# Full-height projections, a split-off negation and a re-ordered plan in a linear-attention kernel with two matrix layers

## The chip, the cores and the metric

The kernel runs on one core of a Trainium2 chip. A core has five engines with a queue of instructions each: TensorE (PE in the profile; its weight loads are PEld) multiplies matrices out of the on-chip memory SBUF into the eight banks of the accumulator memory PSUM; VectorE (DVE) and ScalarE (ACT) do the elementwise work; GpSimd (POOL) here reduces over partitions; SyncE (SP) issues transfers. Engines wait for one another through semaphores. The metric is device time in microseconds.

## The reference

Four batches of eight heads with 576 tokens of 64 numbers pass through an attention with exponential features, then through two dense layers without a bias:

```python
def phi(x):
    proj = np.einsum('bhsd,df->bhsf', x, w_phi)              # 64 -> 128 features
    proj = proj - np.max(np.abs(proj), axis=-1, keepdims=True)
    return np.concatenate([np.exp(proj), np.exp(-proj)], axis=-1)
q_p, k_p = (phi(q), phi(k))
kv = np.einsum('bhsf,bhsd->bhfd', k_p, v)
z = np.sum(k_p, axis=2)
num = np.einsum('bhsf,bhfd->bhsd', q_p, kv)
den = np.einsum('bhsf,bhf->bhs', q_p, z)[..., None] + 1e-06
x = num / den                                                # (2304 tokens, 512)
h = x @ w_in;  x = np.maximum(0.01 * h, h) @ w_out           # layer 1, 512 -> 2048 -> 512
h = x @ w_in2; r = np.maximum(h, 0.0); out = (r * r) @ w_out2
```

The weights of both layers come as 64-bit floats.

## The kernel before

Heads go in pairs: 16 pairs (batch b, pair p), for each of which `k_pair` makes the sums over the keys and `q_pair`, twice, the outputs of half of the tokens (288). Layer 1 (`moe`) goes over five blocks of up to 512 tokens, and in each over 16 pieces of 128 hidden features; it is the longest stretch of matmuls, and attention of batches 1 to 3 runs between its pieces. Layer 2 (`h_unit`, `y_unit`) multiplies by seven products in place of eight, in sweeps over 768 tokens. Weights are turned from 64-bit floats into two rounded halves on DVE and ACT (`w_float`, `w_split`: the tiles `raw`, `wf`, `arena`, `more`, `room`), and products there take three matmuls (high by high, high by low, low by high); those of batch 0 that are called `plain` take one in full precision, which the profile records as two.

In `k_pair` the keys come as a tile of 640 columns: four tiles of 128 tokens with both heads of the pair in the 128 partitions, and a fifth with the 64 left-over tokens of both heads side by side in columns 512 to 639 of partitions 0 to 63; partitions 64 to 127 are zero there. `proj` multiplies tile and weights (`wst`, or its halves `wbh` and `wbl`); for the fifth tile it takes 64 rows. `center` (DVE, lines 1144 and 1145) takes the largest magnitude of each token out of PSUM and negates it, as one step of the plan; `expo` (ACT, line 1151) makes exp(p - max) and exp(max - p) for each head, the tile `kp`; `kv` adds the products of `kp` and the values `vt`. Groups of such tiles are in `KGROUPS`: five groups a pair in batch 0, three in the others.

In `q_pair` the queries `qt` have the same 64 numbers in both halves of the partitions. In batch 0 `proj` multiplies 64 of the rows with `wst`; later `split_a` rounds the whole tile to `qs` (ACT) and `split_b` (DVE) overwrites partitions 64 to 127 with what the rounding lost. Copies `qps`, a reduction over partitions (POOL), exponentials `qe`, their halves, numerator, denominator and its reciprocal (`qden`) follow, and the quotient is split into `xr`, the input of layer 1.

The order of everything is made before the program is: every step is given to a `Plan` with the engines that can take it, an estimated cost and a position. `Plan.order` plays the plan through: each engine, when free, takes the ready step of the lowest position. A step that two engines can take (`{"ACT": (cost, 0), "DVE": (cost, late)}`) counts for the second as so much later. Where TensorE would be idle in the first 95 planned us, `fill` puts a dummy matmul of zeros. The table `P` holds the positions and some costs. What comes out is a fixed sequence for each engine and for SP's queue.

Of the kernel before, what the change touches and what calls it, by code (L numbers as in the profile page):

```python
# [49 lines left out]
P = dict(  # L50
    ring=6, wf=2, raws=3, k0=-165.76, kz=(-19.68, -14.1, -59.35), kp0=15.85, kp=18.51, ks=2.09, kvd=5.48, kb=0, pk=0, pq=0, pn=1, qk=4.25, qk2=11.43,
    q20=-3.11, qd=(1.81, -37.07, 36.76, 8.18, -8.56, -29.92, 30.17), wlead=24.29, wl0=-21.05, ydelay=16.3, xs=(158.38, 39.23, 44.87), xl=58.09,
    xk=58.54, xk2=-16.08, xst=79.13, xld=28.02, lead=37.21, slead=-20.84, w2lead=1.95, ylead=83.28, evac=-13.25, stage0=-49.27, stage=17.12,
    stage2=-17.13, pl=-2.21, c_alt=3.92, sq_alt=14.19, klead=22.1, qlead=14.62, hi_alt=-1.06, dve_alt=42.44, port=1.25, lat=0.125, self=0.115,
    of_pe=0.2, to_pe=0.46, far=0.28, issue=0.47, dma=2.5, rate=320e3, kvc=0.405, switch=0.096, stick=2.0, fill=95, cold=4.98, coldf=2.2,
)
# [185 lines left out]
def attention_moe_moe(ctx: ExitStack, tc: tile.TileContext, qd, kd, vd, wpd, wd, out):  # L242
# [132 lines left out]
    def dves(n, **k):  # L375
        return {"DVE": (on_dve(n, **k), 0)}
# [148 lines left out]
    def stage_pair(p, pos, side):  # L525
# [21 lines left out]

        gate_late.append(plan.add(dves(QD, ops=4), pos - 0.6, comb, r=[f0, f1], w=[sv]))

# [155 lines left out]
    def x_build(i, pos, direct):  # L705
# [6 lines left out]
        for it in range(2 * T // X):  # L712
# [21 lines left out]
            load(512 * 4 * X, pp - P["xl"], get, w=[rv], after=gate_late + need)  # L734
            plan.add(dves(X, ops=4), pp, comb, r=[rv], w=[tv])
            for z, (m0, v, srcs) in enumerate((
# [59 lines left out]
    def h_unit(n):  # L796
# [73 lines left out]
        for c in range(2):  # L870

            def square(e, c=c):
                v = g_tiles[u % UP][:, c]
                if e == "DVE":
                    nc.vector.scalar_tensor_tensor(out=v, in0=v, scalar=0.0, in1=v, op0=ALU.max, op1=ALU.mult)
                else:
                    nc.scalar.activation(out=v, in_=v, func=ACTF.Relu)
                    nc.scalar.activation(out=v, in_=v, func=ACTF.Square)

            plan.add({"ACT": (on_act(2 * T, ops=2), 0), "DVE": (on_dve(2 * T), P["sq_alt"])}, pp + 1 + 0.1 * c, square, p=[g], after=ends[c])  # L880

    def y_unit(n):
# [40 lines left out]
        ops = readers[u % UP]  # L923
        ops.append(plan.add(dves(T, ops=4), pos, comb, r=[gv], w=[sv]))
        for y in range(2):
# [163 lines left out]
    def k_pair(b, p, tpos):  # L1089
# [32 lines left out]
        for tiles, pos in KGROUPS[b > 0]:  # L1122
            pos = tpos[0] + P["ks"] * pos
            heads = [(tt, h) for tt in reversed(tiles) for h in range(1 if tt == 4 else 2)]
# [3 lines left out]
            def proj(e, tiles=tiles, pr=pr):  # L1128
                for y, tt in enumerate(reversed(tiles)):
                    sl, rows, n = (slice(512, 640), slice(0, 64), 128 if plain else 256) if tt == 4 else (slice(tt * 128, (tt + 1) * 128), slice(0, 128), 256)  # L1130
                    ws = [w[rows, 0:n] for w in (wst[:, 128:384], wbh, wbl)]
                    o = banks[pr.bank][:, 256 * y:256 * y + n]
                    if plain:
                        mm(o, t["k"][rows, sl], ws[0], True, True, skip_group_check=True)
                    else:
                        mm(o, t["kh"][rows, sl], ws[1], True, False, skip_group_check=True)
                        mm(o, t["kl"][rows, sl], ws[1], False, False, skip_group_check=True)
                        mm(o, t["kh"][rows, sl], ws[2], False, True, skip_group_check=True)
# [8 lines left out]
            def expo(e, m=m, pr=pr, u=u):  # L1147
                u["kp"] = new("kp", [128, 2, 4, 128], F32)
                for h in range(m):
                    for s, sg in ((0, 1.0), (1, -1.0)):  # L1150
                        nc.scalar.activation(  # L1151
                            out=u["kp"][:, s, h, :], in_=banks[pr.bank][:, h * 128:(h + 1) * 128], func=ACTF.Exp,
                            scale=sg, bias=u["mx"][:, s, h, :],
                        )

# [12 lines left out]

            cost = sum((0.415 if plain else 0.36) if tt == 4 else 0.536 if plain else 0.36 for tt in tiles)
            plan.add(pe(cost), pos, proj, r=[wsv, kt] if plain else [wcv, *ksrc], w=[pr])  # L1170
            plan.add({"DVE": (m * 128 * 1.04e-3 + 0.25, 0)}, pos + 0.4, center, r=[pr], w=[mx]).shared = False
            plan.add({"ACT": (0.5 * m, 0)}, pos + 0.8, expo, r=[pr, mx], w=[kp])
            plan.add(pe((P["kvc"] + 0.02 * (m > 2)) * m), pos + P["kvd"] + P["ks"] * (len(tiles) - 1), kv, r=[kp, vt], w=[acc])
        pos = tpos[-1] + P["kvd"] + 0.1
        f = Value("kvh" if plain_n else "kvf")
# [31 lines left out]
    def q_pair(i, p, pos):  # L1207
        b, c = divmod(i, 2)
        plain, plain_n = b <= P["pq"], b <= P["pn"]
        D8 = P["qd"]  # L1210
        fvals, ft = kvv[b, p]
# [10 lines left out]
        else:  # L1222
# [11 lines left out]
            plan.add(dves(576), pos - 1.5, split_b, r=[qt], w=[qs])  # L1234
        for h in range(2):
            pr = trans(b, False)

            def proj(e, h=h, pr=pr):
                o = banks[pr.bank][:, 0:HALF]
                if plain:  # L1240
                    mm(o, wst[0:64, 0:128], t["q"][0:64, h, :], True, True)
                else:
                    mm(o, w2h, t["qs"][:, h, :], True, False)
                    mm(o, w2l, t["qs"][:, h, :], False, True)
# [5 lines left out]

            plan.add(pe(0.66 if plain else 0.343), pos + D8[0] * h, proj, r=[wsv if plain else wcv, src], w=[pr])
            plan.add({"ACT": (on_act(HALF, psum=True), 0), "DVE": (on_dve(HALF), P["dve_alt"])}, pos + D8[0] * h + 0.2, cp, r=[pr], p=[ps])

# [106 lines left out]
    for b in range(B):  # L1360
        for p in range(PAIRS):
            if b == 0:
                tp = P["k0"] + P["kp0"] * p
            else:
                tp = at[NCH * (b - 1)] + P["kz"][b - 1] + P["kp"] * p
            todo.append((tp - 12, 0, "k", (b, p, [tp + P["ks"] * o for o in range(5)])))
            for c in range(2):
                qp = tp + P["qk"] + P["qk2"] * c + (P["q20"] * c if b == 0 else 0)
                todo.append((qp - 12, 1, "q", (qp, 2 * b + c, p)))
# [92 lines left out]
```

## Time and profile before

| | us |
|---|---|
| median of three runs | 977.25 (975.85 to 987.81) |
| the profiled execution, its own time | 976.32 |
| its span | 974.6 |
| PE busy | 957.0 |
| PEld busy | 862.9 |
| DVE busy | 775.2 |
| ACT busy | 562.0 |
| POOL busy | 92.6 |

The span runs from the first to the last instruction; the rest of the time lies around it. Busy is the time in which an engine had an instruction in work. Matmuls of PE overlap, so PE counts as busy also where they follow each other with small delays. The granted TensorE clock was 0.999 of full speed. A row "out<-in" names the tile written and those read; "64\*128" is rows by columns of the weights, "128x288" the shape written.

### The profile page before, as it was taken

Reading aid. Unit: us, or ns where it says so; the run is one execution under the profiler, and the core shown is the slowest. Engines: PE = TensorE matmul, PEld = TensorE weight load, DVE = VectorE, ACT = ScalarE, POOL = GpSimd, SP = SyncE. Lnnn points to the kernel's source line nnn. Section 1 sums busy time; section 2 is a strip of 40 time slices with the busy share of each in tenths; the row PEclk is TensorE's granted clock in tenths of the full one; section 3 lists DMA queues with packets and bytes.
Section 4 is the critical chain, followed back from the end, with each engine's and each line's share of the span. In section 5 each row is a group of like instructions: output and inputs, shape, how many; then the busy total and the mean of one; then the engine's idle time right before and its main releaser. Section 6 shows DMA issues by size and latency. Waiting matters only on the chain.

```text
span 974.6 us, 16578 instructions
## 1 busy us (share of the span) xinstructions
PE 957.0 (98%) x5893; PEld 862.9 (89%) x5893; DVE 775.2 (80%) x1628; ACT 562.0 (58%) x1327; POOL 92.6 (9%) x52
## 2 busy tenths in 40 slices
PE   9999999999999999999999999999999999999997
PEld 7788877888888888888888899999999999999997
DVE  6999999999999999995143421779997787878877
ACT  7997878678787879863232332344543434334343
POOL 2331201011212101110000000000000000200201
PEclk9999999999999999999999999999999999999999
DMA  8547978987888578799779399979975294818623
GB/s 273 194 143 269 313 237 293 328 285 273 279 280 303 195 243 281 251 300 365 285 256 335 135 311 336 357 301 286 305 295 210 116 335 171 278 28 305 160 76 66
DMA packets 89010, 244.89 MB, mean 251 GB/s; under 512 B 7776, under 2 KB 32224, under 8 KB 85856
## 3 DMA queue, kind: packets, MB, share of 16 engines
q1 hardware_dynamic: 85616, 239.65, 70.6%
q0 software_dynamic: 3312, 4.20, 2.8%
q8 instruction: 46, 0.75, 0.3%
q14 instruction: 36, 0.29, 0.1%
HBM read 167.00 MB, written 76.81 MB: 250 GB/s over the span
## 4 chain that ended last, share of the span: by engine, by line
PE 56%; DVE 31%; DMA 6%; issue 3%; ACT 3%; SPq 0%; DVEq 0%; ACTq 0%
PE bank L348 56%; DVE qden L1326 3%; DVE s L357 3%; DVE gl L357 2%; DMA raw<-wd 2%; DVE wf L483 2%; DVE room L357 2%; DVE g L991 1%; DVE kmx L1144 1%; DVE raw L478 1%; DVE g L835 1%; DMA wid<-room 1%; DVE qm L357 1%; DMA wsd<-arena 1%; DVE qs L357 1%
## 5 line engine op out<-in xcount | busy, mean ns | idle before, releaser
L348 PE MATMUL bank<-gh,arena 128*128 128x512 f32 (+1 forms) x640 | 200.1, 372 | 0.0
L348 PE MATMUL bank<-xr,arena 128*128 128x512 f32 (+1 forms) x720 | 162.9, 370 | 0.0
L357 DVE TENSOR_TENSOR gl<-g,gh 128x512 fp32r<-128x512 f32 (+2 forms) x176 | 94.2, 539 | 75.0 <-ACT gh L352 74.3
L348 PEld LDWEIGHTS bank<-xr,arena 128*128 128x128 f32 x720 | 124.8, 189 | 21.4
L348 PEld LDWEIGHTS bank<-gh,arena 128*128 128x128 f32 x640 | 117.1, 189 | 19.5
L348 PE MATMUL bank<-gl,arena 128*128 128x512 f32 (+1 forms) x320 | 118.0, 369 | 0.0
L1256 POOL PARTITION_ALL_REDUCE qm<-qps x32 | 75.8, 2369 | 342.2 <-ACT qps L352 231.2
L352 ACT ACTIVATE gh<-g 128x512 fp32r<-128x512 f32 (+2 forms) x157 | 77.5, 501 | 38.6 <-PE bank L348 35.2
L1151 ACT ACTIVATE kp<-bank,kmx 128x128 f32<-128x128 f32 x288 | 79.9, 382 | 16.0 <-DVE kmx L1145 14.2
L348 PE MATMUL bank<-xc,w 128*128 128x384 f32 x504 | 88.7, 334 | 0.0
L646 ACT ACTIVATE g<-bank 128x512 f32<-128x512 f32 (+1 forms) x80 | 44.2, 552 | 76.0 <-PE bank L348 75.7
L348 PEld LDWEIGHTS bank<-xc,w 128*128 128x128 f32 x504 | 87.1, 188 | 0.0
L348 PE MATMUL bank<-arena,sc 128*128 128x256 f32 x648 | 83.3, 282 | 0.2 <-DVE g L839 0.2
L352 ACT ACTIVATE sc<-s 128x256 fp32r<-128x256 f32 (+1 forms) x89 | 45.9, 517 | 62.8 <-DVE s L357 23.7
L348 PEld LDWEIGHTS bank<-arena,sc 128*128 128x128 f32 x648 | 79.8, 188 | 0.6 <-issue 0.3
L348 PEld LDWEIGHTS bank<-vt,kp 128*128 128x128 f32 x576 | 69.7, 191 | 6.2 <-ACT kp L1151 1.7
L348 PE MATMUL bank<-vt,kp 128*128 128x65 f32 (+1 forms) x576 | 70.4, 273 | 1.6 <-ACT qden L1312 1.0
L348 PEld LDWEIGHTS bank<-gl,arena 128*128 128x128 f32 x320 | 60.4, 189 | 8.5
L357 DVE TENSOR_TENSOR sc<-s,sc 128x512 fp32r<-128x512 f32 (+1 forms) x96 | 51.3, 553 | 18.8 <-ACT sc L352 18.8
L835 DVE TENSOR_TENSOR g<-bank,g 128x384 f32<-128x384 f32 x72 | 40.0, 555 | 33.1 <-PE bank L348 27.6
L1326 DVE RECIPROCAL qden<-qden 128x288 f32<-128x288 f32 x32 | 62.3, 1946 | 1.2 <-ACT qden L1312 1.1
L352 ACT ACTIVATE g<-bank 128x384 f32<-128x384 f32 (+2 forms) x60 | 29.0, 483 | 57.6 <-PE bank L348 57.6
(141 smaller groups left out, 1873.7 us busy)
## 6 DMA issues: line engine op xcount, KB each, us to landing
arena<-wsd SPq DMA_DIRECT2D x72, 512.0 KB, 5.0
raw<-wd SPq DMA_DIRECT2D x64, 512.0 KB, 5.3
xc<-xcd SPq DMA_DIRECT2D x28, 768.0 KB, 12.9
arena<-wcd SPq DMA_DIRECT2D x10, 1792.0 KB, 7.4
wsd<-arena SPq DMA_DIRECT2D x28, 512.0 KB, 4.8
wid<-room SPq DMA_DIRECT2D x24, 512.0 KB, 5.1
wcd<-room SPq DMA_DIRECT2D x24, 512.0 KB, 4.7
xcd<-xc SPq DMA_DIRECT2D x14, 768.0 KB, 9.2
```

The costliest lines, as they stand in the source:

```text
L348: nc.tensor.matmul(out=o, lhsT=lhsT, rhs=rhs, start=start, stop=stop, **kw)
L352: nc.scalar.activation(out=out, in_=in_, func=ACTF.Copy)
L357: ENG[e].tensor_tensor(out=out, in0=a, in1=b, op=ALU.subtract)
L478: nc.vector.tensor_scalar(out=low, in0=low, scalar1=29, scalar2=None, op0=ALU.logical_shift_right)
L483: nc.vector.scalar_tensor_tensor(out=t["f"].bitcast(I32), in0=high, scalar=3, in1=low, op0=ALU.logical_shift_left, op1=ALU.bitwise_or)
L646: nc.scalar.activation(out=t["g"], in_=banks[hb.bank][:, 0:N], func=ACTF.Prelu, alpha=0.01)
L835: nc.vector.tensor_tensor(out=t[o], in0=m(z), in1=t["a"], op=ALU.add)
L991: nc.vector.tensor_tensor(out=o, in0=a, in1=b, op=op)
L1144: nc.vector.tensor_reduce(out=mx[1], in_=o, axis=AX.X, op=ALU.max, apply_absolute_value=True)
L1151: nc.scalar.activation(out=u["kp"][:, s, h, :], in_=banks[pr.bank][:, h * 128:(h + 1) * 128], func=ACTF.Exp, scale=sg, bias=u["mx"][:, s, ...
L1256: nc.gpsimd.partition_all_reduce(out_ap=t["m"].rearrange("p h s -> p (h s)"), in_ap=t["ps"].rearrange("p h s -> p (h s)"), channels=128, r ...
L1326: nc.vector.reciprocal(out=t["d"], in_=t["d"])
```

## The change

- The fifth tile of the keys, and the queries of batch 0, are projected with all 128 rows; the weights used have zeros in partitions 64 to 127 where those rows hold something else.
- `split_b` writes the lost parts to partitions 0 to 63 and leaves the rounded numbers in 64 to 127.
- `center` keeps the maximum alone; the negation is a step of its own, `negate`, which ACT or DVE can take, and `expo` is two steps, of which the one with exp(max - p) needs no negation.
- Planned costs of these steps and of the four-part combinations change, and nearly all numbers of `P`, some of them now apart for batch 0. Every order follows from these.

```diff
-    ring=6, wf=2, raws=3, k0=-165.76, kz=(-19.68, -14.1, -59.35), kp0=15.85, kp=18.51, ks=2.09, kvd=5.48, ...
+    ring=6, wf=2, raws=3, k0=-171.94, kz=(-21.52, -26.27, -66.22), kp0=15.74, kp=18.04, ks=2.77, kvd=5.48, ...
...
+    ng_alt=20.3, of_pe=0.2, to_pe=0.46, far=0.28, issue=0.47, dma=2.5, rate=320e3, kvc=0.405, switch=0.096, stick=-15.08, fill=95, cold=4.98,
+    coldf=2.2, qd0=(4.31, -14.43, 40.84, 7.57, 13.97, 1.25, 42.32), ks0=1.47, kvd0=2.9, qk0=4.73,
...
-                    sl, rows, n = (slice(512, 640), slice(0, 64), 128 if plain else 256) if tt == 4 else (slice(tt * 128, (tt + 1) * 128), slice(0, 128), 256)
-                    ws = [w[rows, 0:n] for w in (wst[:, 128:384], wbh, wbl)]
+                    sl, n = slice(tt * 128, (tt + 1) * 128), 128 if plain and tt == 4 else 256
+                    ws = [w[:, 0:n] for w in (wst[:, 128:384], wbh, wbl)]
...
                 nc.vector.tensor_reduce(out=mx[1], in_=o, axis=AX.X, op=ALU.max, apply_absolute_value=True)
-                nc.vector.tensor_scalar(out=mx[0], in0=mx[1], scalar1=-1.0, scalar2=None, op0=ALU.mult)
+
+            def negate(e, m=m, u=u):
+                mx = [u["mx"][:, s, 0:m, :] for s in range(2)]
+                if e == "ACT":
+                    nc.scalar.activation(out=mx[0], in_=mx[1], func=ACTF.Copy, scale=-1.0)
+                else:
+                    nc.vector.tensor_scalar(out=mx[0], in0=mx[1], scalar1=-1.0, scalar2=None, op0=ALU.mult)
...
+            def expo(e, s, m=m, pr=pr, u=u):
+                if "kp" not in u:
+                    u["kp"] = new("kp", [128, 2, 4, 128], F32)
                 for h in range(m):
...
-            plan.add({"ACT": (0.5 * m, 0)}, pos + 0.8, expo, r=[pr, mx], w=[kp])
+            plan.add({"ACT": (0.15, 0), "DVE": (0.075, P["ng_alt"])}, pos + 0.6, negate, r=[mx], w=[mn]).shared = False
+            plan.add({"ACT": (0.25 * m, 0)}, pos + 0.7, lambda e, f=expo: f(e, 1), r=[pr, mx], p=[kp])
+            plan.add({"ACT": (0.25 * m, 0)}, pos + 0.8, lambda e, f=expo: f(e, 0), r=[pr, mx, mn], p=[kp])
...
-                sub(e, r[64:128], t["q"][64:128], r[64:128])
+                sub(e, r[0:64], t["q"][0:64], r[0:64])
...
-                    mm(o, wst[0:64, 0:128], t["q"][0:64, h, :], True, True)
+                    mm(o, wst[:, 128:256], t["q"][:, h, :], True, True)
```

In the printed orders TensorE has 250 dummy matmuls for 209 and otherwise the same matmuls; SP's queue has 471 entries in both, POOL's 55, in the same order. DVE has 1,585 instructions for 1,628: 41 of the 56 negations are ACT's now. Of those 56, 20 belong to batch 0, and 13 of these 20 stay on DVE. ACT has 1,372 instructions for 1,327.

DVE at the end of attention of batch 0, before (`kmx` is the maximum, `qden` the denominator, `xr` the input of layer 1, `kl` the lost part of batch 1's keys):

```order
L1326 RECIPROCAL qden<-qden 128x288
L1144 TENSOR_REDUCE kmx<-bank_76 128x4
L1145 TENSOR_SCALAR kmx<-kmx 128x4
L1329 TENSOR_TENSOR qnum<-qnum,qden 128x288
L483 SCALAR_TENSOR_TENSOR wf<-raw 128x512
L354 CAST xr<-qnum 128x256
L354 CAST xr<-qnum 128x32
```

The same place after the change:

```order
L1336 RECIPROCAL qden<-qden 128x288
L1145 TENSOR_REDUCE kmx<-bank_76 128x4
L1339 TENSOR_TENSOR qnum<-qnum,qden 128x288
L484 SCALAR_TENSOR_TENSOR wf<-raw 128x512
L355 CAST xr<-qnum 128x256
L355 CAST xr<-qnum 128x32
```

The negation between the reduction and the quotient has left DVE's sequence; what follows stands as it stood.

ACT at the first keys of batch 1, before (`kp` the exponentials of the keys, six of them for three heads):

```order
L352 ACTIVATE kvh<-bank_82 128x2x64
L352 ACTIVATE qps<-bank_80 128x288
L352 ACTIVATE kvh<-bank_82 128x2x64
L1151 ACTIVATE kp<-bank_76,kmx 128x128 x6
L474 ACTIVATE raw<-raw 128x512
L1312 ACTIVATE qden<-bank_77 64x288
```

The same keys after the change:

```order
L353 ACTIVATE xr<-qnum 128x224
L1150 ACTIVATE kmx<-kmx 128x3
L1158 ACTIVATE kp<-bank_76,kmx 128x128 x3
L1322 ACTIVATE qden<-bank_75 64x288
L1158 ACTIVATE kp<-bank_76,kmx 128x128 x3
L1322 ACTIVATE qden<-bank_77 64x288
```

The negation stands on ACT right before the exponentials, and these are two runs of three with a denominator of batch 0 between them.

TensorE at the beginning of layer 1, before (`xr,arena` is layer 1, `qs,arena` a query projection of batch 1, `vt,kp` the key sums):

```order
L348 MATMUL bank_75<-vt,kp 128x65 x16
L348 MATMUL bank_76<-qs,arena 128x288 x2
L348 MATMUL bank_77<-xr,arena 128x512 x12
L348 MATMUL bank_75<-qs,arena 128x288 x2
L348 MATMUL bank_78<-xr,arena 128x512 x12
```

And after the change:

```order
L349 MATMUL bank_77<-xr,arena 128x512 x6
L349 MATMUL bank_75<-vt,kp 128x65 x4
L349 MATMUL bank_76<-room,kh 128x256
L349 MATMUL bank_76<-room,kl 128x256
L349 MATMUL bank_76<-room,kh 128x256 x2
L349 MATMUL bank_76<-room,kl 128x256
L349 MATMUL bank_76<-room,kh 128x256
L349 MATMUL bank_77<-xr,arena 128x512 x6
```

Pieces of attention now stand between halves of a piece of layer 1, where before they stood between whole ones.

## Rows read from the trace of the kernel before

**Rows 1.** Stretches: from:to, length, busy us (instructions) by engine, clock, DMA share, GB/s.

```profile
20.00:78.00 58.00, 56.48 (x440) 46.91 (x438) 56.34 (x111) 52.69 (x160) 15.97 (x7) 1.00 0.52 175
78.00:440.00 362.00, 355.59 (x1904) 299.60 (x1903) 350.00 (x661) 285.38 (x723) 55.31 (x23) 1.00 0.82 278
160.00:320.00 160.00, 157.80 (x868) 134.58 (x868) 154.68 (x294) 125.41 (x323) 24.28 (x10) 1.00 0.84 286
440.00:640.00 200.00, 200.00 (x1114) 178.86 (x1113) 81.67 (x172) 67.83 (x125) 0.00 (x0) 1.00 0.82 293
640.00:960.00 320.00, 317.93 (x2265) 315.01 (x2264) 264.46 (x622) 138.85 (x272) 13.60 (x13) 1.00 0.63 215
```

**Rows 2.** Waits, 78 to 440 us: engine, for whom, total us, times, longest.

```profile
PEld bank L348 <- ACT kp L1151: 7.1, 12, 1.4
...
PEld bank L348 <- ACT qps L352: 4.2, 8, 1.7
...
PE bank L348 <- ACT kp L1151: 2.6, 4, 1.0
```

**Rows 3.** Timeline of DVE around a negation: start, us, engine, line, operation.

```profile
108.58 0.41 DVE L1144 TENSOR_REDUCE kmx<-bank 128x2 f32<-128x256 f32 x1
109.03 0.17 DVE L1145 TENSOR_SCALAR kmx<-kmx 128x2 f32<-128x2 f32 x1
109.10 0.45 DVE L1329 TENSOR_TENSOR qnum<-qnum,qden 128x288 f32<-128x288 f32 x1
109.47 0.82 DVE L357 TENSOR_TENSOR kl<-kt,kh 128x640 fp32r<-128x640 f32 x1
```

**Rows 4.** Groups by shape, DVE, 0 to 440 us: busy us, mean ns, idle before.

```profile
L1145 DVE TENSOR_SCALAR kmx<-kmx 128x2 f32<-128x2 f32 x28 | 7.4, 265 | 1.0
L354 DVE CAST gh<-g 128x512 fp32r<-128x512 f32 x13 | 6.6, 506 | 0.8 <-ACT g L646 0.8
L354 DVE CAST arena<-wf 128x512 fp32r<-128x512 f32 x8 | 4.6, 581 | 0.0
...
L1145 DVE TENSOR_SCALAR kmx<-kmx 128x4 f32<-128x4 f32 x12 | 3.6, 301 | 0.4
L354 DVE CAST room<-s 128x512 fp32r<-128x512 f32 x7 | 3.5, 495 | 0.0
L1145 DVE TENSOR_SCALAR kmx<-kmx 128x3 f32<-128x3 f32 x12 | 2.9, 242 | 0.4
```

**Rows 5.** Groups by shape, ACT, 0 to 440 us: its smallest operation.

```profile
L352 ACT ACTIVATE xr<-qnum 128x32 fp32r<-128x32 f32 x3 | 0.7, 234 | 1.2 <-DVE qnum L1329 1.2
```

**Rows 6.** Timeline of PE: projections of 64 rows, and products of 128.

```profile
8.78 0.75 PE L348 MATMUL bank<-qt,wst 64*128 64x288 f32 x2
9.46 0.70 PE L348 MATMUL bank<-wst,kt 128*128 128x256 f32 x2
...
53.52 1.23 PE L348 MATMUL bank<-qt,wst 64*128 64x288 f32 x4
54.68 0.38 PE L348 MATMUL bank<-room,kh 128*128 128x256 f32 x1
...
55.78 2.21 PE L348 MATMUL bank<-qe,kvh 128*128 128x288 f32 x8
57.83 1.90 PE L348 MATMUL bank<-vt,kp 128*128 128x65 f32 x16
```

**Rows 7.** Timeline of PE: a key projection of 128 rows, then dummy matmuls.

```profile
63.74 0.50 PE L348 MATMUL bank<-room,kh 128*128 128x256 f32 x1
64.07 0.28 PE L348 MATMUL bank<-room,kl 128*128 128x256 f32 x1
...
64.65 2.69 PE L348 MATMUL bank<-zeros 128*128 128x128 bf16 x45
67.15 0.51 PE L348 MATMUL bank<-qs,arena 128*128 128x288 f32 x2
```

**Rows 8.** Timeline of PE: the first matmuls of layer 1.

```profile
77.68 2.91 PE L348 MATMUL bank<-xr,arena 128*128 128x512 f32 x12
```

More of the change, by code (lines that the diff above doesn't have):

```diff
@@ L546, in comb @@
                 sub("DVE", q[3], a12, q[1])
-        gate_late.append(plan.add(dves(QD, ops=4), pos - 0.6, comb, r=[f0, f1], w=[sv]))
+        gate_late.append(plan.add({"DVE": (on_dve(QD, ops=4) + 0.118, 0)}, pos - 0.6, comb, r=[f0, f1], w=[sv]))
         def part_of(t, a, m):
@@ L734, in x_build @@
             load(512 * 4 * X, pp - P["xl"], get, w=[rv], after=gate_late + need)
-            plan.add(dves(X, ops=4), pp, comb, r=[rv], w=[tv])
+            plan.add({"DVE": (on_dve(X, ops=4) + 0.118, 0)}, pp, comb, r=[rv], w=[tv])
             for z, (m0, v, srcs) in enumerate((
@@ L878, in square @@
                     nc.scalar.activation(out=v, in_=v, func=ACTF.Square)
-            plan.add({"ACT": (on_act(2 * T, ops=2), 0), "DVE": (on_dve(2 * T), P["sq_alt"])}, pp + 1 + 0.1 * c, square, p=[g], after=ends[c])
+            plan.add({"ACT": (on_act(2 * T, ops=2) + 0.13, 0), "DVE": (on_dve(2 * T) + 0.04, P["sq_alt"])}, pp + 1 + 0.1 * c, square, p=[g], after=ends[c])
     def y_unit(n):
@@ L923, in y_unit @@
         ops = readers[u % UP]
-        ops.append(plan.add(dves(T, ops=4), pos, comb, r=[gv], w=[sv]))
+        ops.append(plan.add({"DVE": (on_dve(T, ops=4) + 0.118, 0)}, pos, comb, r=[gv], w=[sv]))
         for y in range(2):
@@ L1167, in kv @@
                         )
-            cost = sum((0.415 if plain else 0.36) if tt == 4 else 0.536 if plain else 0.36 for tt in tiles)
+            cost = sum((0.26 if plain else 0.36) if tt == 4 else 0.536 if plain else 0.36 for tt in tiles)
             plan.add(pe(cost), pos, proj, r=[wsv, kt] if plain else [wcv, *ksrc], w=[pr])
-            plan.add({"DVE": (m * 128 * 1.04e-3 + 0.25, 0)}, pos + 0.4, center, r=[pr], w=[mx]).shared = False
-            plan.add({"ACT": (0.5 * m, 0)}, pos + 0.8, expo, r=[pr, mx], w=[kp])
-            plan.add(pe((P["kvc"] + 0.02 * (m > 2)) * m), pos + P["kvd"] + P["ks"] * (len(tiles) - 1), kv, r=[kp, vt], w=[acc])
-        pos = tpos[-1] + P["kvd"] + 0.1
+            mn = Value()
+            plan.add({"DVE": (m * 128 * 1.04e-3 + 0.07, 0)}, pos + 0.4, center, r=[pr], w=[mx]).shared = False
+            plan.add({"ACT": (0.15, 0), "DVE": (0.075, P["ng_alt"])}, pos + 0.6, negate, r=[mx], w=[mn]).shared = False
+            plan.add({"ACT": (0.25 * m, 0)}, pos + 0.7, lambda e, f=expo: f(e, 1), r=[pr, mx], p=[kp])
+            plan.add({"ACT": (0.25 * m, 0)}, pos + 0.8, lambda e, f=expo: f(e, 0), r=[pr, mx, mn], p=[kp])
+            plan.add(pe((P["kvc"] + 0.02 * (m > 2)) * m), pos + P["kvd0" if b == 0 else "kvd"] + P["ks"] * (len(tiles) - 1), kv, r=[kp, vt], w=[acc])
+        pos = tpos[-1] + P["kvd0" if b == 0 else "kvd"] + 0.1
         f = Value("kvh" if plain_n else "kvf")
@@ L1209, in q_pair @@
         plain, plain_n = b <= P["pq"], b <= P["pn"]
-        D8 = P["qd"]
+        D8 = P["qd0" if b == 0 else "qd"]
         fvals, ft = kvv[b, p]
@@ L1230, in split_b @@
                 r = t["qs"]
-                sub(e, r[64:128], t["q"][64:128], r[64:128])
+                sub(e, r[0:64], t["q"][0:64], r[0:64])
             plan.add(acts(576), pos - 2, split_a, r=[qt], w=[qs])
-            plan.add(dves(576), pos - 1.5, split_b, r=[qt], w=[qs])
+            plan.add({"DVE": (on_dve(576), 0)}, pos - 1.5, split_b, r=[qt], w=[qs])
         for h in range(2):
```

36 lines of the change are left out of this document (16 added, 20 removed).

## The prediction

> **What bounds the kernel now.** Read the stretches first [rows 1]. In each row the second figure is what TensorE (PE) was busy. From 440 to 640 us PE is busy for 200.00 of 200 us and VectorE (DVE) for 81.67: there TensorE alone sets the pace, and from 640 to 960 us it is busy for 317.93 of 320. Before that it is another kernel. From 78 to 440 us DVE is busy for 350.00 of 362 us and from 20 to 78 us for 56.34 of 58, so 97% in both, while ScalarE (ACT) has 285.38 and 52.69. PE is shown busy there too, but its matmuls are pipelined and overlap in the record; the table of waits says more [rows 2]. In 78 to 440 us the weight loads of PE wait 7.1 us for the exponentials `kp`, and 4.2 us for the query copies `qps`, both made by ACT, and the matmuls wait another 2.6 us for `kp`. So the first 440 us are a pipeline in which DVE has hardly a gap, ACT hands its results over late, and PE waits in small pieces. The rest is bare PE work.
>
> Where does the change act? The printed orders agree from the other end: the last 1,860 matmuls of PE and the last 490 instructions of DVE are the same ones in the same order, and before them, with short pieces exchanged between, stand unbroken blocks of 258 and 672 matmuls that reach back into the later part of layer 1. Nothing that the change does reaches the part after 440 us except by when it begins. So the 535 us from there on are taken over as they are, and everything below is a shift of the point at which TensorE is left to run alone.
>
> **The parts, and what each costs.**
>
> *The negated maximum.* Before, DVE reduces a tile, then negates at once: reduce at 108.58 (0.41 us), negation at 109.03, next operation at 109.10 [rows 3]. Neighbours overlap by 0.08 us (109.10 + 0.45 against 109.47), so without the negation the next would start near 108.91: 0.19 us each. Of the 56 negations 41 go to ACT, which makes 41 x 0.19 = 7.8 us off DVE. By the mean durations of the rows, which hold some that were slowed to over a microsecond, it is 16 x 0.265 + 11 x 0.242 + 11 x 0.301 = 10.2 us for the 38 with two or more heads [rows 4]. Those are the two ends.
>
> *What DVE gets in exchange.* The new order sends more rounding copies to DVE. Counted up to the last split of `xr`, which ends attention: 5 more `room<-s` at 0.495, 4 more `arena<-wf` at 0.581, 4 more `gh<-g` at 0.506 [rows 4]: 2.5 + 2.3 + 2.0 = +6.8 us. The other differences there are one to four instructions each, of both signs, and I cost them at nothing, within 1 us. DVE thus loses between 7.8 - 6.8 = 1.0 us and 10.2 - 6.8 = 3.4 us until attention is done. I take **-2.0**, a little under the middle since the row with the start times is the more direct one. As DVE is 97% busy this counts in full.
>
> *Exponentials.* exp(max - x) needs the maximum alone and no longer waits for the negation, which is 0.19 us earlier for its group. 12 + 4 = 16 waits of PE in 78 to 440 us end on `kp` [rows 2]: at most 16 x 0.19 = 3.0 us, at least nothing, if ACT has other work queued ahead. On ACT itself the nearest small operation is 0.234 us (128x32) [rows 5], so 41 cost it at most 9.6 us. What hides them is ACT's idle time, 362 - 285.38 = 77 us from 78 to 440 us. In the prologue there is little of it (5.3 us of 58), but there 13 of the 20 negations stay on DVE, so ACT gets 7 x 0.234 = 1.6 us. If that cover fails, rival B is what follows.
>
> *Full-height projections.* A lone query projection of 64 rows takes from 8.78 to 9.46, 0.68 us; two in a row take from 53.52 to 54.68, 0.58 each; a product of the same width over 128 rows, eight records for four of them, takes from 55.78 to 57.83, 0.51 each [rows 6]. So 0.07 to 0.17 us for each of 16 query projections and 4 left-over key tiles of batch 0: -1.4 to -3.4. For the 12 left-over tiles of the later batches, six matmuls of which three have 64 rows take from 54.68 to 55.78, 1.10 us [rows 6]; six of 128 rows take from 63.74 to 64.65, 0.91 with a late start, and by the later five of them (64.07 to 64.65) 6 x 0.116 = 0.70 [rows 7]: -0.2 to -0.4 each, -2.3 to -4.8. Together -3.7 to -8.2 us of PE, in the stretch where PE waits for others.
>
> The Trainium skill speaks against this part: TensorEngine Tiling (Array Packing), sections Overview and When to Use Tiling, has contractions of up to 64 run as row tiles, for up to twice the rate. The trace doesn't agree: two 64-row projections in a row were slower than two of 128 rows, 1.16 against 1.02 us. By that rule the 16 projections would cost PE 16 x 0.25 = 4 us instead of gaining, an estimate from half of 0.51, and the sum would be near 978.
>
> *Fillers.* 41 more dummy matmuls stand before the first matmul of layer 1 (250 for 209). 45 of them took from 64.65 to 67.15, 0.056 us each [rows 7]: +2.3 us at most, nothing if they only fill waiting. The first x of layer 1 needs DVE's last split of batch 0 anyway, and in DVE's order less work stands before that one than before, by the negations that left.
>
> *Low half of the queries.* The subtraction keeps its shape, 64 partitions by 576, so its time; nothing, and the products summed are the same in another order.
>
> *The rest of the order* has the same instructions and the same transfers in other places. SP's queue has 471 entries in both, with single loads moved by a few places: nothing, unless a load comes late, which is in rival B's price.
>
> **Sum.** PE's own saving becomes waiting time as long as DVE sets the pace, so DVE's -2.0 is the base. The earlier exponentials, with PE's saving behind them, could add between 0 and 3.0; I take half, -1.5. That makes -3.5 us. The profiled execution took 976.3 us (span 974.6, 1.7 around it), so **972.8 us**; the median of the runs shown is 977.25, 0.9 above that execution. The forecast's own range is 967 to 976.
>
> **Rivals.**
>
> *A. The order closes gaps of its own (faster, about 966).* DVE still idles 1.7 + 12.0 = 13.7 us in 20 to 440 us [rows 1]. If the new order removes the later half of that, and PE's saving and the shorter waits let it, the gain is 3.5 + 7 = 10.5: 966; with all of it 959, which is as far as it goes. For it: PE's, ACT's and DVE's terms all point down, and the waits of [rows 2] are on what gets earlier. Against: DVE at 97% has little left, and a fixed order can't be better than its estimates.
>
> *B. ACT becomes late (slower, about 986).* ACT's order has more work than before in front of the middle units of layer 1: negations, and batch 1's attention taken earlier against its weight work. Priced by durations of the same forms it is 4 us more at the end of attention (36 more instructions, of which 41 negations at most 9.6 us, less the rounding copies that went to DVE), but 10 to 14 us more in front of the activations of 160 to 320 us. ACT's idle time there is 160 - 125.41 = 34.6 us [rows 1]. It decides where that idle time is not where the work lands: then matmuls of layer 1 wait for `gh`, PE loses up to 13, and the forecast's 3.5 come off: +9.5, 986. Against it: 34.6 covers 14. For it: PE's waits already end on ACT, not on DVE. The Trainium skill has a rule on this side too: ScalarE: Activation LUTs, section Rules for kernel authors, puts multiplications on VectorE and not on ScalarE.
>
> *C. Nothing comes through (976).* DVE's saving is eaten by the copies it was given, and the first 78 us, where 13 negations stay where they were, set the start of layer 1.
>
> *D. 64-row tiles were the better ones,* by the rule above: 978.
>
> **Chances.** Forecast 0.55, A 0.17, B 0.17, C 0.09, D 0.02. The range must leave out no more than 2 in 10: it takes the forecast, C and D, most of A (to 963) and most of B (to 983): **963 to 983**. A difference of 2%, which is 19.5 us and about what a measurement of this kernel can tell from no change, would need 957.7 or less, beyond all that A has to give unless PE's saving comes on top: 0.03. Slower by as much, 996.8, would need B's price twice over: 0.04. Within 2%: 0.93.
>
> **What would show it.** In the stretches: 440 to 960 us unchanged in kind, all of the difference earlier. DVE's negations 56 to 15, its busy time to attention's end 1 to 4 us less. Waits of PE for `kp` shorter, none on a 64-row form. B would show as waits of PE for `gh` or `qden` growing between 160 and 320 us. The forecast is wrong if the first matmul of layer 1 starts over 3 us earlier or later than at 77.68 [rows 8], if DVE's idle time before 440 us changes by over 5 us, or if any of the difference arises after it.

## The result, and the profile after

The changed kernel takes 963.97 us (median of four runs, 963.57 to 965.49), against 979.2 us for the kernel before in the same series (median of four, 975.85 to 987.81). The ratio, estimated from the fast runs of both and so not the quotient of these medians, is 0.9854 with an interval of 0.9823 to 0.9885. The profiled execution took 963.57 us (span 961.8) for 976.32 (974.6): 12.8 us less. The forecast was 972.8 in a range of 963 to 983. The direction and the range held, the size did not: it said -3.5 from the profiled execution, and -12.8 came.

The stretches of the kernel after, with the columns of [rows 1]:

```profile
20.00:78.00 58.00, 57.88 (x476) 50.73 (x475) 57.41 (x110) 52.56 (x168) 15.35 (x7) 1.00 0.57 181
78.00:440.00 362.00, 356.81 (x1934) 304.75 (x1933) 348.35 (x648) 290.56 (x755) 54.74 (x23) 1.00 0.86 294
160.00:320.00 160.00, 157.71 (x876) 135.71 (x875) 156.94 (x299) 132.00 (x348) 26.46 (x12) 1.00 0.87 302
440.00:640.00 200.00, 200.00 (x1159) 180.76 (x1158) 78.01 (x158) 68.87 (x131) 0.00 (x0) 1.00 0.78 283
```

The share of DVE is what it was: 57.41 of 58 and 348.35 of 362, for 56.34 and 350.00. A full engine stays full while the work in front of it gets less, so the time is found by matching the same instruction in both traces instead. Starts on TensorE, in us (`xr` matmuls are those of layer 1 that read its input):

| | before | after | shift |
|---|---|---|---|
| first matmul of layer 1 | 77.7 | 72.6 | -5.1 |
| 241st of its `xr` matmuls | 243.3 | 241.0 | -2.3 |
| 481st | 424.6 | 415.2 | -9.5 |
| 529th | 448.0 | 436.9 | -11.1 |
| first of layer 2 | 602.6 | 591.6 | -11.1 |
| last matmul of all | 968.44 | 955.35 | -13.1 |

From the 529th on the shift stays constant to the end of layer 1. Between, it goes up and down because the new order puts attention and layer 1 differently. Layer 2 brings another 2 us.

The waits of the kernel after, 78 to 440 us (engine, for whom, total us, times, longest), first of the weight loads, then of the matmuls:

```profile
PEld bank L349 <- ACT kp L1158: 3.2, 5, 1.6
...
PE bank L349 <- ACT kp L1158: 0.5, 2, 0.3
```

Against [rows 2] the waits for `kp` went from 7.1 + 2.6 to 3.2 + 0.5 us, and those for `qps` from 4.2 to 2.1.

What the negation costs on ACT stands in its timeline (start, us, engine, line, operation):

```profile
105.95 0.19 ACT L1150 ACTIVATE kmx<-kmx 128x3 f32<-128x3 f32 x1
106.04 0.87 ACT L1158 ACTIVATE kp<-bank,kmx 128x128 f32<-128x128 f32 x3
```

It is busy for 0.19 us, but the exponentials start 0.09 us after its own start, since neighbours overlap. The forecast priced it at up to 0.234 from [rows 5].

Full-height projections of queries in the kernel after, alone and two in a row, for those of [rows 6]:

```profile
9.83 0.70 PE L349 MATMUL bank<-qt,wst 128*128 128x288 f32 x2
10.37 1.00 PE L349 MATMUL bank<-vt,kp 128*128 128x65 f32 x8
11.20 0.70 PE L349 MATMUL bank<-qt,wst 128*128 128x288 f32 x2
...
50.58 1.19 PE L349 MATMUL bank<-qt,wst 128*128 128x288 f32 x4
51.61 0.44 PE L349 MATMUL bank<-zeros 128*128 128x128 bf16 x5
```

From start to start one takes 0.54 us (0.68 before) and two take 1.03 (1.16 before). All sixteen together, each to the start of the next other instruction, took 9.81 us before and 8.41 after: -1.4, the low end of the forecast's -1.4 to -3.4 that it gave for queries and plain key tiles together. The matmuls beside a 64-row one take longer too, which neither the forecast nor this sum counts (last section).

### The profile page after: what moved, and what is told of

It is laid out like the page before. It is cut to its first block, busy times and chain, and to the rows that moved or that the text cites. A ratio compares the mean times of both kernels' runs of the same rounds, so it can differ in the third digit from the quotient of the medians.

```text
span 961.8 us, 16628 instructions
## 1 busy us (share of the span) xinstructions
PE 946.5 (98%) x5934; PEld 864.2 (90%) x5934; DVE 762.4 (79%) x1585; ACT 566.7 (59%) x1372; POOL 91.2 (9%) x52
## 4 chain that ended last, share of the span: by engine, by line
PE 59%; DVE 26%; ACT 5%; DMA 5%; issue 3%; SPq 0%; DVEq 0%; ACTq 0%
PE bank L349 59%; DVE qden L1336 3%; DMA raw<-wd 3%; DVE gl L358 2%; DVE wf L484 2%; DVE s L358 2%; DVE room L358 2%; DVE qs L358 1%; DVE g L992 1%; DVE kmx L1145 1%; ACT kp L1158 1%; DVE arena L358 1%; ACT qe L1282 1%; DVE qel L358 1%; DVE raw L479 1%
## 5 line engine op out<-in xcount | busy, mean ns | idle before, releaser
L353 ACT ACTIVATE gh<-g 128x512 fp32r<-128x512 f32 (+2 forms) x152 | 74.5, 498 | 39.0 <-PE bank L349 36.2
L1158 ACT ACTIVATE kp<-bank,kmx 128x128 f32<-128x128 f32 x288 | 84.4, 380 | 2.4 <-issue 1.7
L349 PE MATMUL bank<-arena,gh 128*128 128x256 f32 x324 | 60.8, 283 | 1.3 <-DVE xt L992 1.3
```

Source lines behind the costliest of these rows:

```text
L349: nc.tensor.matmul(out=o, lhsT=lhsT, rhs=rhs, start=start, stop=stop, **kw)
L353: nc.scalar.activation(out=out, in_=in_, func=ACTF.Copy)
L1158: nc.scalar.activation(out=u["kp"][:, s, h, :], in_=banks[pr.bank][:, h * 128:(h + 1) * 128], func=ACTF.Exp, scale=1.0 - 2.0 * s, bias=u[" ...
```

## The experiments

Ratios are to the kernel before, timed in the same series; times are medians. "Shift" is a start in the trace against the kernel after, as in the table. The medians of the kernel before were 977.09 to 979.2 in the five series, so a difference to the kernel after of under 2 us shows little by itself. A shift is that of one execution, which can be the fastest or the slowest of its kernel. Unless one says otherwise, a kernel keeps the order of the kernel it starts from, instruction by instruction.

### Order or operations?

**New operations in the old order.** The kernel before, with full-height projections and the low half, the negation on ACT for batches 1 to 3, and the exponentials exp(max - p) ahead of the others of their group:

```diff
-                nc.vector.tensor_scalar(out=mx[0], in0=mx[1], scalar1=-1.0, scalar2=None, op0=ALU.mult)
+                if b == 0:
+                    nc.vector.tensor_scalar(out=mx[0], in0=mx[1], scalar1=-1.0, scalar2=None, op0=ALU.mult)
...
+                if b > 0:
+                    nc.scalar.activation(out=u["mx"][:, 0, 0:m, :], in_=u["mx"][:, 1, 0:m, :], func=ACTF.Copy, scale=-1.0)
```

> The order of the kernel before, with the operations of the change in it: 128 rows for the left-over keys and batch 0's queries, the low half of the queries, the negation on ACT for batches 1 to 3 (on DVE in batch 0), exp(max - x) ahead of exp(x - max). Theory ORDER (most of the gain comes from the new sequence): 3 us or less are gained, 973 to 977. Rival OPS (the operations themselves bring it): 7 us or more, 969 or less.

969.57 us, ratio 0.9923 (0.9905 to 0.9941), before 977.58: -8.0 without any new order. In its trace the gain grows from 0.7 us at the first matmul of layer 1 to 3.2 at the 241st and 8.2 at the 481st, and stays there; layer 2 takes 0.6 back.

**Old operations in the new order.** The kernel after with the 64-row projections, the high half and the negation in `center` on DVE (`negate` does nothing):

```diff
+                nc.vector.tensor_scalar(out=mx[0], in0=mx[1], scalar1=-1.0, scalar2=None, op0=ALU.mult)
...
-                    mm(o, wst[:, 128:256], t["q"][:, h, :], True, True)
+                    mm(o, wst[0:64, 0:128], t["q"][0:64, h, :], True, True)
...
-                sub(e, r[0:64], t["q"][0:64], r[0:64])
+                sub(e, r[64:128], t["q"][64:128], r[64:128])
```

> The order of the change, with the operations of before in it: 64 rows, the high half, all 56 negations on DVE right behind their maximum. Theory ORDER: 7 us or more of the 12 remain, 969 or less. Rival OPS: it falls back to 973 or more.

975.64 us (median of twelve), 0.9973 (0.9957 to 0.9989): the order alone brings 1.9 us. In the traces, layer 2 from its first to its last matmul takes 365.8 us in the kernel before and 364.1 here, so about 1.7 us of it lie there. Read the other way, the operations are worth 975.64 - 963.97 = 11.7 us in the new order.

**New operations planned with the old table.** The kernel after, planned anew with the numbers of `P` from before (the separate numbers of batch 0 set to the common ones):

```diff
-    ring=6, wf=2, raws=3, k0=-171.94, kz=(-21.52, -26.27, -66.22), ...
+    ring=6, wf=2, raws=3, k0=-165.76, kz=(-19.68, -14.1, -59.35), ...
```

> The change's operations, steps and planned costs with the numbers of the table from before (batch 0's separate numbers set to the common ones, the delay of a negation on DVE as in the change): the order is planned anew from them. Theory TABLE (what the sequence adds to the operations' 8 us, some 5 us, comes from the new numbers): 968 to 971. Rival STEPS (it comes from the negation and the exponentials being steps of their own, and from better costs): 966 or less.

972.51 us, 0.9945 (0.9927 to 0.9963), 8.5 slower than after, and slower also than the new operations in the old order. Its plan has 372 dummy matmuls for 250. The new numbers are worth little with the old operations (1.9) and much with the new ones (8.5): they fit the new operations better. "Order" and "operations" aren't terms that add up.

### Which operation?

**Only the 64-row projections back**, queries and left-over keys, in the kernel after:

```diff
-                        mm(o, t["kh"][:, sl], ws[1], True, False, skip_group_check=True)
+                        mm(o, t["kh"][rows, sl], ws[1], True, False, skip_group_check=True)
...
-                    mm(o, wst[:, 128:256], t["q"][:, h, :], True, True)
+                    mm(o, wst[0:64, 0:128], t["q"][0:64, h, :], True, True)
```

> The change with its 64-row projections put back (16 query projections, 16 left-over key tiles), everything else and the order as in the change. Theory ORDER: TensorE waits in that part anyway, so 0 to +2 us on the change's 964. Rival OPS: +4 us or more, the rows' own 3.7 to 8.2 us in full.

968.86 us, 0.991 (0.989 to 0.9929): +4.9. The first matmul of layer 1 starts at 76.07 for 72.62, +3.5; after that the shift grows only to 4.1. As both traces hold the same matmuls in the same order, the shift can be told apart by where it arises (us, by the start in the kernel after):

| stretch | at 64-row matmuls and their two neighbours | at all others |
|---|---|---|
| 7.4 to 20 | +1.6 | 0.0 |
| 20 to 72.6 | +2.8 | -1.1 |
| 72.6 to 415 | +4.3 | -3.7 |

So the 64 rows cost TensorE 8.7 us. Up to layer 1, 3.3 of 4.4 us stay in the time; after it, beside attention of the later batches, only 0.6 of 4.3, since other matmuls then follow their neighbours sooner.

**Only the left-over key tiles back to 64 rows:**

```diff
-                        mm(o, t["kh"][:, sl], ws[1], True, False, skip_group_check=True)
+                        mm(o, t["kh"][rows, sl], ws[1], True, False, skip_group_check=True)
```

> The change with the left-over key tiles alone put back to 64 rows (16 tiles, 48 matmuls or records of the later batches among them); batch 0's queries keep 128. All rows put back cost 4.9 us, 3.5 of them before layer 1 began. Theory PROLOGUE (TensorE is close to the limit in the first 73 us, and the 16 query projections there carry most): +0.5 to +2 us on 964. Rival COUNT (it goes by the matmuls' own time, of which the 12 later tiles have 2.3 to 4.8 us): +3 us or more.

965.54 us, 0.9877 (0.9861 to 0.9893): +1.6, with the first matmul of layer 1 at 73.37. Of the 3.5 us there, 2.7 are thus the query projections of batch 0. What they are worth at the end isn't settled: by the medians 4.9 - 1.6 = 3.3 us, but the trace of this kernel, the slowest of its five runs, is 3.3 us late at layer 2 where that of all rows is 4.1, which leaves 0.8.

**Only the negation back on DVE**, in `center`:

```diff
+                nc.vector.tensor_scalar(out=mx[0], in0=mx[1], scalar1=-1.0, scalar2=None, op0=ALU.mult)
...
-            def negate(e, m=m, u=u):
+            def negate(e):
+                pass
```

> The change with the negation back on DVE right behind each maximum, everything else and the order as in the change; DVE gets 41 instructions of 0.19 us back, 7.8 us. Theory ORDER: +1 to +4 us on the change's 964, since DVE still has gaps to take them. Rival OPS, by which DVE's work counts in full: +6 us or more.

968.83 us, 0.9912 (0.9894 to 0.993): +4.9. Its shift is +1.1 at the first matmul of layer 1 and grows to +5.4. The two single steps, 4.9 + 4.9 = 9.8, nearly make up the 11.7 of all the operations.

### What does a microsecond cost on each engine?

In the kernel after, work was added whose result nobody uses. **On DVE**, a second negation for each of the 36 groups of batches 1 to 3 (36 x 0.19 = 6.8 us by [rows 3]):

```diff
                 nc.vector.tensor_reduce(out=mx[1], in_=o, axis=AX.X, op=ALU.max, apply_absolute_value=True)
+                if b > 0:
+                    nc.vector.tensor_scalar(out=dead[:, 0:m].rearrange("p (a b) -> p a b", b=1), in0=mx[1], scalar1=-1.0, scalar2=None, op0=ALU.mult)
```

> The change with 36 dead negations on DVE, one behind each maximum of batches 1 to 3, into a tile that nobody reads; ACT's negations stay. 36 x 0.19 = 6.8 us of DVE. Theory TURNS (before 440 us DVE, PE and ACT hold each other up in turn, and work on any of them costs half or more of itself): +3.5 us or more on the change's 964. Rival LATENCY (what putting the negation back cost, 4.9 us, was exponentials that start later): 0 to +1.5 us, as nobody waits for these.

970.51 us, 0.9922 (0.9906 to 0.9938). **On ACT**, 68 negations, two for each group of batches 1 to 3 whose own negation is there (68 x 0.09 = 6 us):

```diff
+                    if b > 0:
+                        for y in range(2):
+                            nc.scalar.activation(out=dead[:, 4 * y:4 * y + m].rearrange("p (a b) -> p a b", b=1), in_=mx[1], func=ACTF.Copy, scale=-1.0)
```

> The change with 68 dead negations on ACT, two behind each of its 34 negations of batches 1 to 3; they take 0.09 us each between their neighbours, 6 us of ACT. Theory TURNS: +3 us or more on 964. Rival ROOM (ACT idles over 70 us from 78 to 440 us and takes such work for nothing): 0 to +1.5 us.

966.89 us, 0.9882 (0.9864 to 0.99). Both hold an error of the edit: the new 32-byte tile `dead` moved other tiles, and layer 1 itself became slower (last section). They were run again, writing into padding that was there already:

```diff
-    dead = const.tile([128, 8], F32, name="dead")
...
-    first.tile([128, EDGE], F32, name="edge")
+    dead = first.tile([128, EDGE], F32, name="edge")
```

> The 36 dead negations on DVE once more (6.8 us of it), now written into a padding tile that was there already, so that nothing moves in SBUF. In the first such run layer 1's matmuls ran 1.8 ns slower each even where neither DVE nor ACT had anything to do with them, about 2 us of its +6.5. Theory TURNS: +3.5 to +5.5 us on the change's 964, and none of it after 430 us. Rival LATENCY: 0 to +1.5 us.

> The 68 dead negations on ACT once more (6 us of it), written into the padding tile. Theory TURNS: +3 us or more on 964. Rival ROOM: 0 to +1.5 us, since about 2 us of the first run's +2.9 arose in the stretch of matmuls alone, from the shift in SBUF.

DVE: 969.54 us, 0.9913 (0.9892 to 0.9934), +5.6 for 6.8 us. ACT: 964.67 us, 0.9869 (0.9852 to 0.9887), +0.7 for 6 us, which can't be told from nothing. Their shifts at layer 2 are +6.6 and 0.0. So ACT has room for such pieces, and DVE hasn't.

**On PE**, each split key projection of batches 1 to 3 repeats its first matmul (60 x 0.12 = 7.2 us by [rows 7]):

```diff
                         mm(o, t["kh"][:, sl], ws[1], True, False, skip_group_check=True)
+                        mm(o, t["kh"][:, sl], ws[1], True, False, skip_group_check=True)
```

> The change with the first matmul of each key projection of batches 1 to 3 made twice (the second overwrites the first): 60 matmuls of 256 columns at 0.12 us, 7.2 us of PE. Theory TURNS: +3.6 us or more on 964. Rival DVE ALONE (the prediction's: PE's work turns into or out of waiting while DVE sets the pace): 0 to +1.5 us.

968.17 us, 0.9897 (0.9879 to 0.9914): +4.2 (shift at layer 2 +5.4, in the slowest of its five runs). TensorE counts too, before 440 us, where DVE is as good as full (348.35 of 362 us in the kernel after). **Dummy matmuls:** of the 250, 106 were left out:

```diff
+        made[0] += 1
+        if made[0] > 38 and made[0] % 2:
+            return
```

> The change with 144 dummy matmuls for 250, every second one after the first 38 left out: 106 x 0.056 = 5.9 us of PE less in the first 73 us. Theory TURNS for the beginning too: layer 1 starts 1 to 4 us earlier, 960 to 963. Rival COVER (they only fill waiting): within 0.5 us of the change's 964.

965.55 us, 0.9873 (0.9853 to 0.9892), +1.6, with intervals of after and this one that overlap. The first matmul of layer 1 comes 0.3 us later, not earlier: the dummies don't hold the start up.

### The rounding copies

The forecast set 6.8 us of copies, which the new order gives to DVE, against the negations that leave it. With the order held fixed, they were given to ACT at the same places: first the `room` copies (14 before 425 us, 6.6 us by their rows), then also those of `arena` (12, 5.4 us), and, apart, the 15 negations still on DVE; last all of it.

```diff
-                copy(e, dst[:, :, 0].bitcast(F32R), src())
+                copy("ACT", dst[:, :, 0].bitcast(F32R), src())
...
-            copy(e, dst()[:, 0].bitcast(F32R), t["f"])
+            copy("ACT", dst()[:, 0].bitcast(F32R), t["f"])
...
-                if e == "ACT":
-                    nc.scalar.activation(out=mx[0], in_=mx[1], func=ACTF.Copy, scale=-1.0)
-                else:
-                    nc.vector.tensor_scalar(out=mx[0], in0=mx[1], scalar1=-1.0, scalar2=None, op0=ALU.mult)
+                nc.scalar.activation(out=mx[0], in_=mx[1], func=ACTF.Copy, scale=-1.0)
```

> The kernel after, in its own order; the rounding copies room<-s and room<-wf that its plan gave to DVE (14 of them before 425 us, 6.6 us by their rows) are emitted for ACT at the same places. Theory (these copies cost what other DVE work costs, 0.8 of their length, and ACT has room at 0.1 to 0.2 of 14 x 0.55): 5.3 - 1.2 = 4.1 us off, about 960. Rival (the planner put them where DVE would have waited anyway, so they cost nothing): 964 to 965. Second rival (ACT is late at those places): over 966.

> As the one with the room copies, and the 12 copies arena<-wf on DVE (5.4 us by their rows) are emitted for ACT as well: 12 us less on DVE, about 14 us more on ACT before 425 us. Theory (0.8 of DVE's work counts, 0.1 to 0.2 of ACT's): 9.6 - 2.1 = 7.5 us off, about 956.5. Rival (the copies sit in gaps of DVE): 964 to 966. Second rival (ACT is late, matmuls of layer 1 wait for arena): 967 to 975.

> The kernel after, in its own order; the 15 negations that its plan left on DVE are emitted for ACT at the same places. DVE gets 15 x 0.19 = 2.9 us less, ACT 15 x 0.09 = 1.4 us more. Theory (DVE's work before 440 us counts at about 0.8, ACT's at 0.1 to 0.2): 2.3 - 0.3 = 2.0 us off the kernel after, about 962. Rival (13 of them lie in the first 78 us, where ACT is as full as DVE and each result is awaited at once): no gain or up to 1.5 us lost, 964 to 965.5.

> Copies and negations of the kernel after all on ACT, at the same places in the order: 15 us less on DVE, 15.5 us more on ACT before 425 us. Theory: the sum of the two, about 954 to 955. Rival (copies in gaps, negations as in the rival there): 964 to 967. Second rival (ACT late): 967 to 977.

`room`: 965.63 us, 0.9883 (0.9867 to 0.9899), +1.7. Both kinds: 968.66 us, 0.991 (0.9895 to 0.9925), +4.7. The 15 negations: 964.67 us, 0.987 (0.9856 to 0.9885), +0.7, no difference that can be told. All: 969.12 us, 0.9917 (0.9902 to 0.9932), +5.2. The shift at the first matmul of layer 2 says the same: +1.0, +4.1, +0.8, +5.5. Nothing is gained by moving 12 us off the fullest engine. The kernel with both kinds of copies on ACT shows why, in the waits of DVE from 20 us to its last split of `xr`, which ends attention:

```profile
DVE room L358 <- ACT room L353: 3.4, 9, 0.6
DVE gh L355 <- ACT g L647: 2.5, 3, 1.7
```

The step that takes the lost part of `room` is on DVE and now waits for the copy from ACT, and other steps of DVE wait for an ACT that is later. In the kernel after, neither wait is over 0.3 us up to there. DVE up to that last split, in all of these traces (us):

| kernel | last split of `xr` | DVE busy until then | DVE idle |
|---|---|---|---|
| before | 434.35 | 413.74 | 20.61 |
| new operations, old order | 425.52 | 403.91 | 21.61 |
| old operations, new order | 433.92 | 414.35 | 19.57 |
| new operations, old table | 431.22 | 404.43 | 26.79 |
| after | 420.70 | 404.54 | 16.16 |
| after, negation back on DVE | 426.55 | 409.94 | 16.61 |
| after, 64 rows back | 424.84 | 406.41 | 18.43 |
| after, copies on ACT | 425.04 | 397.28 | 27.76 |

The new operations take about 9.8 us of work off DVE in either order, and the negation is 5.4 of it. The new order takes off nothing (414.35 for 413.74); with the new operations it lets DVE idle less. With the copies on ACT, DVE works 7.3 us less and idles 11.6 more. Not shown is whether those copies would be dear on ACT in an order made for it.

No kernel was faster than the changed one.

## Why the prediction was right or wrong

*What bounds the kernel.* It took DVE as the only pace before 440 us, from rows that begin at 20 us. This is the first stretch of the kernel before, which it did not read:

```profile
0.00:20.00 20.00, 18.51 (x112) 14.41 (x113) 11.75 (x33) 13.21 (x39) 4.91 (x7) 1.00 0.84 269
```

DVE is busy for 11.75 of 20 us there and PE for 18.51. The kernel after, and then the same order with 64-row projections, show where TensorE has nothing to do: it waits for a transfer, or it has a dummy matmul.

```profile
7.52 0.75 PE L349 MATMUL bank<-qt,wst 128*128 128x288 f32 x2 [1.23 <-DMA qt<-qd]
...
16.45 0.67 PE L349 MATMUL bank<-zeros 128*128 128x128 bf16 x9
```

```profile
18.18 0.67 PE L349 MATMUL bank<-zeros 128*128 128x128 bf16 x9
```

In the kernel after TensorE waits 1.23 us for the first queries, which the other one spends in dummies and key projections that take longer; the query projections then start at 7.52 and 7.66 us. From there neither shows idle time of TensorE up to the dummies at 16.45 and 18.18: 64-row tiles cost 1.6 us in 9, and all of it is time. From 20 us to layer 1 they cost another 2.8 us, of which 1.7 are left at the start of layer 1. There TensorE was the path, and the forecast's rows begin after the part where this is plainest.

*"PE's own saving becomes waiting time as long as DVE sets the pace"*: this step failed first. Of -3.7 to -8.2 us the forecast took nothing into its base and let PE share 1.5 us with the exponentials; undone, the rows cost 4.9 us. The saving itself was 8.7 us in the trace, as a change between 64 and 128 rows costs at the neighbours too. The step is right only for layer 1's stretch, where 3.7 of 4.3 us were made up at other matmuls, and not before it. It isn't firm there either: with the left-over keys alone at 64 rows it was 1.7 of 4.3, and added matmuls, most of them in that stretch, cost 4.2 of 7.2 us (0.6).

*The DVE term, -2.0*: mis-sized. DVE's work up to the end of attention fell by 413.74 - 404.54 = 9.2 us. That 41 negations leave was right; undone, they put 5.4 us of work back and cost 4.9. The copies that were set against them came in the number forecast, but not at 6.8 us. The kernel after has up to there (for 13 `gh` of 6.6 us and 8 `arena` of 4.6 [rows 4], and 6 `room` of 3.0):

```profile
L355 DVE CAST gh<-g 128x512 fp32r<-128x512 f32 x17 | 7.1, 416 | 0.3 <-ACT g L647 0.3
L355 DVE CAST room<-s 128x512 fp32r<-128x512 f32 x11 | 5.7, 519 | 0.0
L355 DVE CAST arena<-wf 128x512 fp32r<-128x512 f32 x12 | 5.4, 447 | 0.0
```

That is +4.0 us, and other pieces of the new order took most of it off DVE again: with the old operations its work is 414.35 us for 413.74. The forecast counted the copies that came and put the rest of the exchange at nothing. It also left out that the other new operations take some 4 us off DVE, by the table above; which of them does so beyond the rows (1.9) isn't shown.

*Earlier exponentials, 0 to 3.0, taken -1.5*: not borne out as a gain. The waits for `kp` fell by 6.0 us, twice the bound, but the negation is not the reason. The kernel with all old operations in the new order waits for `kp` in 78 to 440 us only this long:

```profile
PEld bank L349 <- ACT kp L1155: 2.5, 6, 0.5
```

It takes 975.64 us all the same. With the negation alone back on DVE the waits are 2.7 + 0.2 us, and the kernel is 4.9 slower; the new operations in the old order wait 5.6 + 1.8 and gain 8.0. The new order shortens these waits, and they did not set the time. The dead negations on DVE, whose results nobody awaits, cost 5.6 for 6.8 us as well.

*ACT's price and rival B* (986): the bound of 41 x 0.234 = 9.6 was the busy time of one operation; between neighbours it is 41 x 0.09 = 3.7. ACT's busy time from 160 to 320 us did rise, 125.41 to 132.00, and 68 more operations cost 0.7 us or nothing. That cover held, for small pieces.

*Fillers at nothing*: held. *Low half at nothing*: not run by itself; rows and negation leave 11.7 - 9.8 = 1.9 us for it, for the split of the exponentials and for what they have in common.

*"Nothing after 440 us but by when it begins"*: right for 440 to 640 us, 200.00 busy in both, and wrong by 2 us in layer 2. From 640 us on, weight loads of the kernel before wait among others like this:

```profile
PEld bank L348 <- DVE g L835: 1.5, 4, 0.4
PEld bank L348 <- DVE gl L357: 0.9, 1, 0.9
```

In the kernel after, the four waits for `g` and the one for `gl` are gone; those for `xt` are 2.5 us in both, those for `sc` 0.6 for 0.2. It goes with the order: from its first to its last matmul layer 2 takes 365.8 us before, 366.4 with the new operations in the old order and 366.3 with the old table, but 363.8 after and 363.7 to 364.4 in twelve of the fourteen other kernels in the new order, the one with old operations among them (364.8 and 365.7 in the other two). The sequences of PE and DVE are the same over its last 1,860 matmuls; the PSUM banks that their products use differ, and so do the sequences of ACT and of SP's queue. Which of these ends the waits wasn't tried.

*Rival A* (966, chance 0.17) has the size that came, but not for its reason: the order alone gave 1.9, though its numbers are worth 8.5 together with the operations. It asked for 7 us less idling of DVE; up to the end of attention 4.5 came, and 1.0 with the old operations. That 963.97 lies within the range at all, at its edge, is owed to A, for which the range was drawn down to 963: that much is luck. *Rival C* fell. *Rival D* fell: in one order, 64 rows were 4.9 us slower than 128. By the Trainium skill's TensorEngine Tiling (Array Packing), section When to Use Tiling, contractions of up to 64 are to be run as row tiles; for one that isn't packed with another, these traces don't agree, and no run here has two side by side. On DVE, 96% busy from 78 to 440 us, the negation cost 4.9 us, and 68 more of them on ACT 0.7 or nothing. The Trainium skill's ScalarE: Activation LUTs, section Rules for kernel authors, keeps multiplications on VectorE; by that rule the negations would have stayed on DVE, and here the kernel gained by moving them.

Two of the three signs that the forecast named for being wrong came: the first matmul of layer 1 came 5.1 us earlier, more than 3, and 2 us arose after 440. The third did not: DVE's idle time from 20 to 440 us was 13.7 and is 14.2, as the end of attention moved within that window.

## What to carry to other kernels

Where two or three engines hand small pieces to each other, price an edit on each by what a dose of work costs there (here, by medians, 0.8 us for a us of DVE, 0.6 of TensorE, 0.1 or nothing of ACT) and not by which of them is fullest; here the full engine turned only a part of another's saving into waiting. Read the stretches from the first microsecond: the prologue had another bound than the 400 us that follow. When an order moves work both ways between engines, sum all of the exchange up to the same instruction, and look at what waits for a piece that changes its engine. A wait that gets shorter is no gain until the end of the stretch moves with it.

## What the runs showed of the hardware

**A 32-byte tile that moves others made layer 1 slower.** The two dose kernels with the new tile took 2.3 us more between the 481st and the 769th `xr` matmul, where nothing of their edit runs, and 0.4 less from there to the last. The matmuls of 480 to 570 us by shape (busy us, mean ns, idle), of the dose on DVE with the new tile, and of the dose on DVE without it:

```profile
L350 PE MATMUL bank<-xr,arena 128*128 128x512 f32 x108 | 26.8, 396 | 0.0
```

```profile
L349 PE MATMUL bank<-xr,arena 128*128 128x512 f32 x108 | 26.1, 389 | 0.0
```

From the start of one 512-column matmul of this stretch to the next it is 227.3 ns on average in the kernel after and 229.0 in both with the tile, where about four in ten take 230 or more, for one in ten in the kernel after. By which address it goes was not looked into. An experiment that adds a tile has to look at a stretch that its edit doesn't touch.

**A change between 64 and 128 rows costs TensorE, not the 64 rows.** With the order of the kernel after and 64-row projections, the products between two query projections shown above for the kernel after run like this:

```profile
10.25 0.75 PE L349 MATMUL bank<-qt,wst 64*128 64x288 f32 x2
10.93 1.11 PE L349 MATMUL bank<-vt,kp 128*128 128x65 f32 x8
11.97 0.75 PE L349 MATMUL bank<-qt,wst 64*128 64x288 f32 x2
```

From one query projection to the next it is 1.72 us for 1.37: 0.14 more in the projection and 0.21 in the 128-row products behind it. Over the 27 runs of 64-row matmuls in this trace the median addition, from start to start, is 0.09 us for the matmul before a run, 0.10 for its first, 0.09 for its last and 0.10 for the one behind it. It is nothing for the 22 matmuls inside a run, which have 64-row ones on both sides.
